# A long causal convolution with top-128 routing on one core: a wider unit memory, weighted sums in two accumulators, contiguous copies, and every transfer on one queue

## The chip, the core and the metric

The kernel runs on one core of a Trainium2 chip. The core has a matrix engine (PE, whose weight loads are listed apart as PEld), a vector engine (DVE), an activation engine (ACT), a general engine (POOL) and a sync engine (SP) that only issues transfers. Each engine works through its own instructions in order and waits at semaphores for the others. The metric is the device time of one execution in microseconds; less is better.

## The reference, cut to what matters

```python
batch, seq, d_model = (8, 6336, 128)          # x: 8 x 6336 x 128, h: 6336 x 128
def _attn_ref(x, h):                          # causal convolution along the sequence, per feature
    L = 2 * S
    Xf = np.fft.rfft(x, n=L, axis=1)
    Hf = np.fft.rfft(h, n=L, axis=0)
    return np.fft.irfft(Xf * Hf[None], n=L, axis=1)[:, :S, :]
def _moe_ref(x, w_gate, w1, w2, capacity):    # capacity 128, w1: 128 x 1024, w2: 1024 x 128
    scores = np.einsum('bsd,d->bs', x, w_gate)
    out = x.copy()
    for b in range(B):
        top_idx = np.argpartition(-scores[b], capacity)[:capacity]
        xe = x[b, top_idx]
        ye = np.maximum(xe @ w1, 0.0) @ w2
        g = 1.0 / (1.0 + np.exp(-scores[b, top_idx]))
        out[b, top_idx] = x[b, top_idx] + g[:, None] * ye
    return out
```

The convolution of eight sequences with one filter per feature comes first. Then, for each sequence, the 128 rows with the highest gate score go through a small two-layer network and are written back.

## The kernel before

The sequence length is 6336 = 99 * 64, and the transforms are done as matrix products with tables, in fp32, first over 99 points and then over 64. The work is cut into eight **units**: unit i holds two sequences (2 * (i // 2) and the next) and one half of the features (64 columns). All units go through the same four stages:

- **stage a** (`stage_a`, L121): a group of input columns, folded by POOL (`fold`, L108 and L109: two tensor operations per group), times the table `fa`; the result leaves PSUM by two ACT copies (L127) and two DVE copies (L129) into the unit's spectrum `ys`. Eight groups per unit. The PSUM tiles come from the pool `pb`, which has two buffers.
- **stage b** (`stage_b`, L153): for a chunk of eight of the 99 frequencies, `over_k` multiplies the spectrum by the table `wb` (64 PE instructions per full chunk, into a `pb` tile); then `times` multiplies by the filter's spectrum: four DVE products (L161) out of PSUM, and two POOL additions (L171), which write the result back into the same place of the spectrum. Thirteen chunks per unit, the last one of three frequencies.
- **stage c** (`stage_c`, L231): 64 columns of the spectrum times the table `wc` (16 PE instructions for every two of the 66 steps), and ACT copies (L236), four columns at a time, into `z`. In the same loop DVE adds up the **weighted sum** of all columns (`weigh`, L208 and L210), from which the gate scores come.
- **stage d** (`stage_d`, L264): 16 items of eight PE instructions with the table `at`, one ACT copy each (L269), and one store of the output.

Spectrum, z and the table chunks of stage b share one tile, `slots`, of two slots. Unit i uses slot i % 2: the spectrum lies in the last 12672 numbers of a lane's 16384, z overwrites it from the front while stage c consumes it, and the first 3072 numbers hold three chunks of `wb`:

```python
flat = cp.tile([128, 2 * ZS], F32, name="slots")
ys = [flat[:, (r + 1) * ZS - YS:(r + 1) * ZS].rearrange("p (j k t) -> p j k t", k=N1, t=2) for r in range(2)]
zs = [flat[0:N1, r * ZS:(r + 1) * ZS].rearrange("p (j m t) -> p j m t", m=128, t=2) for r in range(2)]
```

The order of the work is written out by hand, and a layer below it adds a semaphore wait wherever two instructions touch the same part of a tile. First come stage a of the filter and of unit 0, then stage b of both, chunk by chunk (`stage_b_first`, which also copies the filter's spectrum by ACT, L192, and stores it by ACT's queue, L198). From there on, unit i runs stages c and d while unit i + 1 runs stages a and b: the 33 **items** of unit i (17 of stage c with four steps each, 16 of stage d) are emitted one after the other, and ahead of items 1, 3, 5 and 7 stand two groups of stage a, ahead of items 10, 14, 18, 22 and 26 a **pair** of chunks of stage b, ahead of item 30 the last three. After every item one step of the **routing** is emitted (`routes`): scores (L288), a search for the threshold in 16 rounds of one small matmul (L345) and some DVE work (L333 to L350), the gather, and the network for the picked rows (L461, L469). A pair of sequences is complete after two units, so the search runs in stage d of units 1, 3, 5 and 7, and what is left of the routing in stage c of units 2, 4 and 6, and after the last unit.

Two details of the order matter below. `weigh` is emitted ahead of step s until `2 * s + 6` columns are weighed, so all 64 stand in the first half of stage c. And the transfers stand in two queues: SP issues all loads (`load_x` L101, `load_w` L139, `load_h` L145, `load_at` L247), and ACT, between its copies, the output stores (L274, one item late by way of `flush`) and the stores of L198. Each of eight semaphores for transfers is used in turn, so the ninth transfer waits for the first one's end.

## Time and profile before

| | |
|---|---|
| three runs | 1562.04, 1570.03 (median) and 1576.72 us |
| profiled execution | 1568.27 us, of which the span from the first to the last instruction is 1566.5 us |
| mean granted clock of PE | 0.79 of full speed |
| busy share of the span | PE 72%, PEld 62%, DVE 51%, POOL 29%, ACT 21% |
| moved by DMA | 170.81 MB, 109 GB/s over the span |

The span has these stretches: 0 to 51 us stage a of the filter and unit 0; 51 to 137 us the first stage b; then unit by unit stage c and stage d, beginning with unit 0 (137 to 231 and 231 to 308 us); the last unit has nothing to prepare (1434 to 1466 and 1466 to 1521 us), and the last routing ends at 1566.5 us. A share of busy time over the whole span says little here, since the stretches have different limits. What a stretch is worth is read from its own windows and waits.

### The profile page before, as it was taken

To read this page: it belongs to the slowest core of one execution; us is meant where nothing else is said; L and a number is where in the kernel's file an instruction comes from. 1 tells how busy PE (TensorE), PEld (TensorE's weight loads), DVE (VectorE), ACT (ScalarE), POOL (GpSimd) and SP (SyncE) were. 2 spreads that over 40 slices of the span, in tenths; PEclk is the share of its full clock that TensorE was granted. 3 is DMA by queue.
4 is the path that set the end of the run, shared out by engine and by line. 5 is a ranking of instruction groups with operands and counts; after the bars stand their busy time and mean duration, and the time that the engine had idled before them with its cause. 6 is when DMAs were issued, how large, how long until landed. Compare 5 with 4: busy or idle time off the path is not lost.

```text
span 1566.5 us, 39581 instructions
## 1 busy us (share of the span) xinstructions
PE 1122.1 (72%) x17336; PEld 967.9 (62%) x17336; DVE 797.1 (51%) x1927; ACT 329.6 (21%) x603; POOL 459.7 (29%) x371
## 2 busy tenths in 40 slices
PE   6766676767777677766776857767776776777984
PEld 5665575557556576556755757656755666666754
DVE  5436823483466822266274863238446584236552
ACT  3211221132111221123210222103311122113310
POOL 4334323342223233242223223333222223331001
PEclk8997798888775788988886678888888577888855
DMA  7574235432444223542352422434244401252120
GB/s 243 165 236 138 82 86 165 126 121 79 119 120 125 70 58 100 165 140 81 93 148 74 128 59 83 128 112 152 81 114 133 125 18 46 69 166 69 51 83 7
DMA packets 102344, 170.81 MB, mean 109 GB/s; under 512 B 10814, under 2 KB 80028, under 8 KB 102172
## 3 DMA queue, kind: packets, MB, share of 16 engines
q1 hardware_dynamic: 67324, 134.79, 29.0%
q10 hardware_dynamic: 33824, 32.45, 6.6%
q8 instruction: 136, 2.23, 0.6%
q0 software_dynamic: 1024, 1.05, 0.3%
q14 instruction: 36, 0.29, 0.1%
HBM read 135.29 MB, written 32.96 MB: 107 GB/s over the span
## 4 chain that ended last, share of the span: by engine, by line
PE 53%; DVE 26%; POOL 12%; issue 5%; DMA 2%; ACT 1%; POOLq 0%; SPq 0%; DVEq 0%; ACTq 0%
PE pb L153 17%; PE pa L264 17%; DVE acc L210 14%; PE pa L231 11%; POOL slots L171 10%; PE pb L121 4%; DVE slots L129 3%; DVE tx L161 3%; PE m L461 1%; PE m L469 1%; DVE cmp L333 1%; DMA at<-tab_at 1%; POOL xr L109 1%; DVE slots L161 1%; DVE num L337 1%
## 5 line engine op out<-in xcount | busy, mean ns | idle before, releaser
L153 PE MATMUL pb<-slots 128*64 128x64 f32 x6336 | 282.2, 262 | 242.4 <-POOL slots L171 242.3
L171 POOL TENSOR_TENSOR slots<-slots,tx 128x512 f32<-128x512 f32 (+1 forms) x208 | 265.4, 1297 | 629.9 <-DVE tx L161 620.9
L153 PEld LDWEIGHTS pb<-slots 128*64 128x64 f32 x6336 | 265.4, 176 | 260.8 <-POOL slots L171 251.0
L161 DVE TENSOR_TENSOR slots<-pb,ht 128x512 f32<-128x512 f32 (+1 forms) x182 | 120.2, 660 | 437.4 <-PE pb L153 437.2
L264 PE MATMUL pa<-slots,at 99*99 99x256 f32 (+1 forms) x1056 | 310.3, 456 | 8.8 <-ACT slots L236 4.9
L231 PE MATMUL pa<-wc,slots 64*99 64x128 f32 x4096 | 301.7, 304 | 2.3 <-POOL slots L171 1.8
L231 PEld LDWEIGHTS pa<-wc,slots 64*99 64x99 f32 x4096 | 282.3, 191 | 18.1 <-issue 9.0
L210 DVE SCALAR_TENSOR_TENSOR acc<-slots,wgl,acc 128x198 f32<-128x198 f32 x504 | 276.7, 550 | 19.6 <-POOL slots L171 3.4
L264 PEld LDWEIGHTS pa<-slots,at 99*99 99x99 f32 x1056 | 201.0, 203 | 88.4 <-DMA at<-tab_at 7.6
L121 PE MATMUL pb<-fa,xr 50*64 50x99 f32 x2304 | 159.0, 296 | 131.8 <-DVE slots L129 81.1
L236 ACT COPY slots<-pa 99x512 f32<-99x512 f32 x256 | 160.0, 629 | 408.7 <-PE pa L231 393.6
L121 PEld LDWEIGHTS pb<-fa,xr 50*64 50x64 f32 x2304 | 136.7, 167 | 148.3 <-issue 98.5
L269 ACT COPY yt<-pa 99x512 f32<-99x512 f32 x128 | 75.0, 586 | 589.3 <-PE pa L264 314.6
L121 PE MATMUL pb<-fa,xo 50*64 50x99 f32 x2304 | 157.8, 297 | 2.1 <-issue 2.1
L121 PEld LDWEIGHTS pb<-fa,xo 50*64 50x64 f32 x2304 | 133.7, 166 | 2.2 <-issue 2.2
L108 POOL TENSOR_TENSOR xo<-xr 128x512 f32<-128x512 f32 x55 | 71.2, 1294 | 200.4 <-PE pb L121 200.4
L161 DVE TENSOR_TENSOR tx<-pb,ht 128x512 f32<-128x512 f32 (+1 forms) x182 | 119.0, 654 | 0.0
L129 DVE COPY slots<-pb 128x396 f32<-128x396 f32 x144 | 74.9, 563 | 81.0 <-PE pb L121 81.0
L109 POOL TENSOR_TENSOR xr<-xr 128x512 f32<-128x512 f32 x72 | 91.6, 1273 | 33.1 <-DVE xo L108 27.4
L127 ACT COPY slots<-pb 128x396 f32<-128x396 f32 x144 | 66.9, 522 | 122.9 <-PE pb L121 122.9
L435 POOL DMA_INDIRECT xe<-out,iu x16 | 16.1, 1008 | 154.3 <-DVE col L424 151.9
L333 DVE SCALAR_TENSOR_TENSOR cmp<-r,q,quarters 99x192 bf16<-99x192 f32 x128 | 54.7, 469 | 0.3
(95 smaller groups left out, 448.4 us busy)
## 6 DMA issues: line engine op xcount, KB each, us to landing
slots<-tab_wb SPq DMA_DIRECT2D x96, 512.0 KB
xr<-in_x SPq DMA_DIRECT2D x64, 512.0 KB
out<-yt ACTq DMA_DIRECT2D x128, 198.0 KB
ht<-hd SPq DMA_DIRECT2D x84, 256.0 KB
at<-tab_at SPq DMA_DIRECT2D x128, 153.1 KB
hd<-slots ACTq DMA_DIRECT2D x24, 256.0 KB
xr<-in_h SPq DMA_DIRECT2D x8, 512.0 KB
slots<-tab_wb SPq DMA_DIRECT2D x8, 192.0 KB
```

The source lines that it names most:

```text
L108: eng.tensor_tensor(out=odd[g], in0=t[:, 1], in1=t[:, 0], op=ALU.subtract)
L109: pool.tensor_tensor(out=t[:, 0], in0=t[:, 0], in1=t[:, 1], op=ALU.add)
L121: pe.matmul(pt[c * 64:c * 64 + 64, b, d * N1:(d + 1) * N1], src, fa[rows, c], start=True, stop=True)
L129: v.tensor_copy(out=dst[:, b, j:j + 2], in_=src[:, b])
L153: pe.matmul(banks[c][g * 64:g * 64 + 64, j * 64:j * 64 + 64], wt[:, j, c * 64:c * 64 + 64], y[:, :, g, :, k0 + j], start=True, stop=True)
L161: v.tensor_tensor(out=dst, in0=banks[c][:, 0:kn * 64].rearrange("p (k b j t) -> p k b j t", k=kn, b=2, t=2), in1=ht[t].rearrange("p k (j t ...
L171: pool.tensor_tensor(out=d3, in0=d3, in1=tx.rearrange("p k (j t) -> p k j t", t=2), op=ALU.add if c else ALU.subtract)
L210: v.scalar_tensor_tensor(out=acc[:, b], in0=col, scalar=w, in1=acc[:, b], op0=ALU.mult, op1=ALU.add)
L231: pe.matmul(banks[g][0:N1, c % 4 * 128:c % 4 * 128 + 128], y[rows, c // 2, ri, :, c % 2], wc[rows, ri], start=(ri == 0), stop=(ri == 1))
L236: act.copy(out=z[:, c // 2 - 1:c // 2 + 1, g].rearrange("p j m t -> p j t m"), in_=banks[g][0:N1].rearrange("p (j t m) -> p j t m", j=2, t=2))
L264: pe.matmul(pt[0:N1, o:o + w * 128], ats[tau // 2][:, tau % 2, c], z[:, c, q:q + w], start=(c == 0), stop=(c == 1))
L269: act.copy(out=yt.rearrange("p b q d -> p q b d"), in_=pt[0:N1].rearrange("p (q b d) -> p q b d", q=4, b=2))
```

## The change

Six things change.

1. The tile `slots` gets 100 more numbers (400 bytes) in each lane. Nothing is stored in them.
2. `acc` is doubled: columns of even and odd number (t = 0 and 1) are added up in sums of their own, and the scores' first matmul (`scores`) adds the two, with 16 PE instructions in the place of eight.
3. `weigh` is emitted until `s + 5` columns are weighed, one per step, so the 64 are spread over 59 of the 66 steps.
4. z of four columns is one run of 512 numbers rather than two of 256, by another order of the features (`_features`, on the host's side of the layout); so g = 0 no longer holds back its last copy.
5. The products `tx` have three buffers rather than two.
6. The output stores and the stores of the filter's spectrum are issued by SP rather than ACT. They keep their places in the program's order.

```diff
-    flat = cp.tile([128, 2 * ZS], F32, name="slots")
+    flat = cp.tile([128, 2 * ZS + 100], F32, name="slots")
...
-    acc = cp.tile([128, 2, 2, N1], F32, name="acc")
+    acc = cp.tile([128, 2, 2, 2, N1], F32, name="acc")
...
-            tx = tp.tile([128, KC, 64], F32, tag="t", name="tx", bufs=2)[:, 0:kn]
+            tx = tp.tile([128, KC, 64], F32, tag="t", name="tx", bufs=3)[:, 0:kn]
...
-            act.dma_start(out=hd[u, :, :, k0:k0 + kn], in_=hs[:, :, u, 0:kn])
+            sp.dma_start(out=hd[u, :, :, k0:k0 + kn], in_=hs[:, :, u, 0:kn])
...
-        if u == 0 and d == 0:
-            v.tensor_scalar(out=acc[:, b], in0=col, scalar1=w, scalar2=None, op0=ALU.mult)
+        dst = acc[:, t, b]
+        if u == 0 and d < 2:
+            v.tensor_scalar(out=dst, in0=col, scalar1=w, scalar2=None, op0=ALU.mult)
         else:
-            v.scalar_tensor_tensor(out=acc[:, b], in0=col, scalar=w, in1=acc[:, b], op0=ALU.mult, op1=ALU.add)
+            v.scalar_tensor_tensor(out=dst, in0=col, scalar=w, in1=dst, op0=ALU.mult, op1=ALU.add)
...
-        z = zs[r].rearrange("p (j g) m t -> p j g m t", g=2)
+        z = zs[r].rearrange("p (n g j) m t -> p n g j m t", g=2, j=2)
...
-            while weighed < min(64, 2 * s + 6):
+            while weighed < min(64, s + 5):
...
-                c = cols[g] if s < 63 else 63 if s == 65 else -1
+                c = cols[g]
                 if 0 <= c < 64 and c % 4 == 3:
-                    act.copy(out=z[:, c // 2 - 1:c // 2 + 1, g].rearrange("p j m t -> p j t m"),
+                    act.copy(out=z[:, c // 4, g].rearrange("p j m t -> p j t m"),
...
-                act.dma_start(out=out[2 * p:2 * p + 2, u, :, 4 * n:4 * n + 4].rearrange("b a q d -> a b q d"), in_=yt)
+                sp.dma_start(out=out[2 * p:2 * p + 2, u, :, 4 * n:4 * n + 4].rearrange("b a q d -> a b q d"), in_=yt)
...
-                pe.matmul(pt[0:N1, b * 128:(b + 1) * 128], acc[:, b, ri], wc[:, ri], start=(ri == 0), stop=(ri == 1))
+                for t in range(2):
+                    pe.matmul(pt[0:N1, b * 128:(b + 1) * 128], acc[:, t, b, ri], wc[:, ri],
+                              start=(ri + t == 0), stop=(ri + t == 2))
```

What this does to the order shows at three places. The first is the pair of chunks of stage b ahead of item 10 of unit 0, on PE (`pb` is the PSUM tile of a chunk, the names in brackets are the semaphores waited for: DMAHW for a load, DVE and Pool for those engines). Before:

```order
L153 MATMUL pb<-slots 64x64 [waits DMAHW6_49,DVE_49]
L153 MATMUL pb<-slots 64x64 [waits DVE_49]
L153 MATMUL pb<-slots 64x64 x30
L153 MATMUL pb<-slots 64x64 [waits DMAHW7_49,Pool_49]
L153 MATMUL pb<-slots 64x64 x31
```

Now:

```order
L153 MATMUL pb<-slots 64x64 [waits DMAHW6_49]
L153 MATMUL pb<-slots 64x64 [waits DVE_49]
L153 MATMUL pb<-slots 64x64 x30
L153 MATMUL pb<-slots 64x64 [waits DMAHW7_49]
L153 MATMUL pb<-slots 64x64 x31
```

The second chunk waited for POOL, which writes the first chunk's result into other frequencies of the same spectrum; it now waits for its load alone. The same wait is gone from every chunk of the kernel; where a `pb` tile is still in use, the wait is for DVE's products of the chunk before the last.

The second place is DVE's queue in the front of stage c of unit 0: the weighings (L210 before, L211 now) around the copies of the last two stage a groups (ahead of item 7), up to the first product of stage b (ahead of item 10). Before:

```order
L210 SCALAR_TENSOR_TENSOR acc<-slots,wgl,acc 128x198 [waits DVE_49] x16
L129 COPY slots<-pb 128x2x2x99 [waits PE_49]
L129 COPY slots<-pb 128x2x2x99
L129 COPY slots<-pb 128x2x2x99 [waits PE_49]
L129 COPY slots<-pb 128x2x2x99
L210 SCALAR_TENSOR_TENSOR acc<-slots,wgl,acc 128x198 [waits DVE_49] x4
L161 TENSOR_TENSOR slots<-pb,ht 128x8x32x2 [waits DMAHW1_49,PE_49,Activation_49]
L161 TENSOR_TENSOR tx<-pb,ht 128x512
```

Now (L209 begins a new sum):

```order
L211 SCALAR_TENSOR_TENSOR acc<-slots,wgl,acc 128x198 [waits DVE_49] x8
L129 COPY slots<-pb 128x2x2x99 [waits PE_49]
L129 COPY slots<-pb 128x2x2x99
L129 COPY slots<-pb 128x2x2x99 [waits PE_49]
L129 COPY slots<-pb 128x2x2x99
L209 TENSOR_SCALAR acc<-slots,wgl 128x198 x2
L211 SCALAR_TENSOR_TENSOR acc<-slots,wgl,acc 128x198 [waits DVE_49] x10
L161 TENSOR_TENSOR slots<-pb,ht 128x8x32x2 [waits DMAHW7_49,PE_49,Activation_49]
```

Ahead of these copies stand eight weighings where 16 stood. Before, all 64 were done ahead of the first product of stage b; now 44 are, 16 more stand between the first pair of chunks and the second, and the last four behind that.

The third place is SP's queue in stage d of unit 0, from a pair of chunks on. Before:

```order
L139 DMA slots<-tab_wb 128x1024 [waits DMAHW6_49,PE_49]
L145 DMA ht<-hd 128x2x256 [waits DMAHW7_49,DMAHW0_49,DVE_49]
L139 DMA slots<-tab_wb 128x1024 [waits DMAHW0_49,PE_49]
L145 DMA ht<-hd 128x2x256 [waits DMAHW3_49,DMAHW2_49,DVE_49]
L247 DMA at<-tab_at 99x396 [waits DMAHW3_49,PE_49]
L247 DMA at<-tab_at 99x396 [waits DMAHW5_49,DMAHW1_49,PE_49]
```

Now:

```order
L139 DMA slots<-tab_wb 128x1024 [waits DMAHW6_49,PE_49]
L145 DMA ht<-hd 128x2x256 [waits DMAHW7_49,DVE_49]
L139 DMA slots<-tab_wb 128x1024 [waits DMAHW0_49,PE_49]
L145 DMA ht<-hd 128x2x256 [waits DMAHW1_49,DVE_49]
L248 DMA at<-tab_at 99x396 [waits DMAHW2_49,PE_49]
L275 DMA out<-yt 99x2x256 [waits DMAHW3_49,Activation_49]
L248 DMA at<-tab_at 99x396 [waits DMAHW4_49,PE_49]
L275 DMA out<-yt 99x2x256 [waits DMAHW5_49,Activation_49]
```

A store that waits for an ACT copy now stands between every two loads of `at`.

4 lines of the change are left out of this document (2 added, 2 removed).

## The prediction

> **What bounds the kernel now.** I read the chain of work that ended last first (section 4 of the page), then a table of windows by stage, then the waits, then timelines of PE and DVE in the stages that the chain names. The chain's shares by engine and line:
>
> ```profile
> PE 53%; DVE 26%; POOL 12%; issue 5%; DMA 2%; ACT 1%; POOLq 0%; SPq 0%; DVEq 0%; ACTq 0%
> PE pb L153 17%; PE pa L264 17%; DVE acc L210 14%; PE pa L231 11%; POOL slots L171 10%; PE pb L121 4%; DVE slots L129 3%; DVE tx L161 3%; PE m L461 1%; PE m L469 1%; DVE cmp L333 1%; DMA at<-tab_at 1%; POOL xr L109 1%; DVE slots L161 1%; DVE num L337 1%
> ```
>
> PE does not lead alone: POOL's additions of stage b (L171) and DVE's weighings (L210) stand on the path with 24% between them. The windows by stage show how long each stretch is (length, then busy time of PE, PEld, DVE, ACT, POOL, then the granted clock and the DMA share):
>
> ```profile
> 51.00:137.00 86.00, 54.44 (x1596) 52.45 (x1587) 32.47 (x57) 13.96 (x28) 32.47 (x26) 0.92 0.58 188
> 231.00:308.00 77.00, 54.27 (x669) 43.59 (x669) 25.48 (x43) 9.28 (x16) 24.94 (x20) 0.84 0.45 131
> 308.00:395.00 87.00, 62.09 (x1280) 58.01 (x1280) 51.31 (x90) 27.75 (x49) 28.53 (x22) 0.84 0.38 114
> 395.00:492.00 97.00, 69.88 (x692) 55.03 (x693) 53.66 (x178) 9.10 (x16) 25.01 (x20) 0.72 0.37 106
> 492.00:604.00 112.00, 80.20 (x1352) 72.82 (x1351) 65.14 (x161) 30.32 (x59) 34.63 (x28) 0.76 0.31 89
> 1434.00:1466.00 32.00, 31.09 (x515) 29.67 (x513) 23.32 (x56) 20.56 (x33) 0.00 (x0) 1.00 0.11 32
> ```
>
> These are the first stage b, stage d of unit 0, stages c and d of unit 1 (d with the search), stage c of unit 2 (with the rest of the routing), and stage c of unit 7, which has neither stage a nor b beside it and no POOL work. There the 512 instructions of stage c take 32 us at full clock; beside stages a and b the same work takes 87 to 112 us, with PE busy 62 to 80. In every stretch before the last unit some 20 us or more of PE are idle. The waits say where:
>
> ```profile
> PE pb L153 <- POOL slots L171: 242.3, 61, 5.9
> PE pb L121 <- DVE slots L129: 81.1, 20, 5.4
> ```
>
> **The wait for POOL.** A pair of chunks in stage c of unit 1, and one in stage d of unit 0, on PE (start, length, count, and in brackets the idle time ahead with its releaser):
>
> ```profile
> 362.65 2.10 PE L153 MATMUL pb<-slots 128*64 128x64 f32 x64
> 369.02 3.53 PE L153 MATMUL pb<-slots 128*64 128x64 f32 x64 [4.27 <-POOL slots L171]
> 372.49 7.58 PE L231 MATMUL pa<-wc,slots 64*99 64x128 f32 x128
> 379.99 2.10 PE L153 MATMUL pb<-slots 128*64 128x64 f32 x64
> ...
> 257.92 3.68 PE L153 MATMUL pb<-slots 128*64 128x64 f32 x64 [4.18 <-POOL slots L171]
> 261.53 7.96 PE L264 MATMUL pa<-slots,at 99*99 99x256 f32 x32
> 269.42 2.10 PE L153 MATMUL pb<-slots 128*64 128x64 f32 x64
> ```
>
> The second chunk waits some 4.2 us for products and additions of the first, and then runs 3.53 to 3.68 us where the first ran 2.10: the pause has halved the clock. So a removed wait is worth 4.2 us plus about 1.4 of slow clock, 5.6 us. The order shows that the change removes it everywhere (the 61 waits are 12 in the first stage b and seven in each of units 0 to 6). What comes next is the second chunk's load, issued two chunks earlier, and the `pb` tile, free since the chunk before the last.
>
> In the first stage b the wait is shorter, once per chunk:
>
> ```profile
> 59.38 2.10 PE L153 MATMUL pb<-slots 128*64 128x64 f32 x64 [2.37 <-POOL slots L171]
> 61.32 2.04 PE L153 MATMUL pa<-slots 128*64 128x64 f32 x64
> ```
>
> Twelve of 2.37 us are 28 us. DMA moves there at a share of 0.58 of 86 us, 50 us of work, which the shorter stretch must still hold with the spectrum's stores now in one queue with the loads. I take **22 us** (ends: 0 if the transfers bind at today's pace, 36 if PE's 50 us alone do).
>
> In stage d the three pairs and the last three chunks of a unit lose 3 x 5.6 + 2 x 4.2 + 1.4 = 26.6 us; seven units, **186 us**. DVE (four products a chunk) and POOL hide under the items of stage d that follow.
>
> **The front of stage c.** DVE leads there. One cycle of two items in unit 1 and, by its copies alone, in unit 2:
>
> ```profile
> 329.08 10.20 DVE L210 SCALAR_TENSOR_TENSOR acc<-slots,wgl,acc 128x198 f32<-128x198 f32 x16
> 339.20 1.04 DVE L129 COPY slots<-pb 128x396 f32<-128x396 f32 x2
> 342.07 1.05 DVE L129 COPY slots<-pb 128x396 f32<-128x396 f32 x2 [1.83 <-PE pb L121]
> 343.03 10.11 DVE L210 SCALAR_TENSOR_TENSOR acc<-slots,wgl,acc 128x198 f32<-128x198 f32 x16
> ...
> 516.61 1.04 DVE L129 COPY slots<-pb 128x396 f32<-128x396 f32 x2
> 532.83 1.04 DVE L129 COPY slots<-pb 128x396 f32<-128x396 f32 x2
> ```
>
> Weighings alone in unit 7, and the line's shortest, median and longest (ns):
>
> ```profile
> 1435.91 23.32 DVE L210 SCALAR_TENSOR_TENSOR acc<-slots,wgl,acc 128x198 f32<-128x198 f32 x51
> ```
> ```profile
> L210 DVE SCALAR_TENSOR_TENSOR acc<-slots,wgl,acc x504: 406/425/1541, 139.4 to 1458.8; 128x198 f32<-128x198 f32 x168
> ```
>
> The cycle is 343.03 - 329.08 = 13.95 us, 16.2 with routing. A weighing costs 0.457 us with POOL idle (23.32 / 51), of which a part is the wait for the one before it, since all add to one sum; the 16 of a cycle take 10.20 us, not 7.3, because POOL's four folds run meanwhile: single weighings then last up to 1541 ns. The copies, which PE waits for, stand behind them. Two sums take some of the dependence away; no row shows weighings without it. I bound the new step by the shortest one, 0.406, and today's 0.457, and take 0.42. Eight fewer weighings are 3.7 us and the shorter step 0.3: 4.0 us a cycle in the four units without routing, where the folds still block the eight that stay. With routing DVE spends more of the cycle on other work, so I let half of the blocking (1.45 of 2.9 us) go as well: 5.5 us. Four cycles each: 4 x 4 x 4.0 + 3 x 4 x 5.5 = **130 us** (ends: 0 if DVE's other work fills the room; 190 if no fold blocks any more, when copies of 2.1, PE's 1.8 and eight weighings of 0.406 make a cycle of 7.2 us, 6.8 less, in 28 cycles).
>
> **The back of stage c.** From pair to pair is 379.99 - 362.65 = 17.34 us today. Without the wait PE needs 2 x 2.1 + 7.58 = 11.8. But DVE now has 16 weighings between the pairs, and POOL's additions meet them:
>
> ```profile
> L161 DVE TENSOR_TENSOR slots<-pb,ht 128x512 f32<-128x512 f32 (+1 forms) x182 | 120.2, 660 | 437.4 <-PE pb L153 437.2
> L171 POOL TENSOR_TENSOR slots<-slots,tx 128x512 f32<-128x512 f32 (+1 forms) x208 | 265.4, 1297 | 629.9 <-DVE tx L161 620.9
> ```
>
> Eight products of 0.66, 16 x 0.42, and one POOL addition of 1.3 that is still running when the weighings begin: 13.3 us. The z copies wait for weighings, so PE follows: 17.3 - 13.3 = 4.0 us a pair, 14 pairs, **56 us** (ends: 0, and 5.6 x 14 = 78). Here a rule speaks against the change. The Trainium skill (SBUF — State Buffer, section Who interferes with whom) says that a DVE instruction with two SBUF inputs contends with a POOL instruction that reads SBUF, and that the later one waits until the earlier is done. The maximum of L210 agrees with it: 1541 ns is 1135 over the minimum, less than one POOL operation of 1297. If all eight additions of the two pairs blocked by that rule rather than two, the sum would be 7 x 6 x 1.3 = 55 us longer.
>
> **The search in stage d.** Units 1, 3 and 5, on PE:
>
> ```profile
> 452.98 1.96 PE L264 MATMUL pa<-slots,at 99*99 99x256 f32 x8
> 457.53 0.24 PE L345 MATMUL m<-num,ones 99*99 99x6 bf16 x1 [2.60 <-DVE num L337]
> 457.63 3.71 PE L264 MATMUL pa<-slots,at 99*99 99x256 f32 x8
> ```
>
> Unit 7's search, as a window:
>
> ```profile
> 1480.00:1500.00 20.00, 20.00 (x52) 13.10 (x52) 9.62 (x48) 2.93 (x5) 0.00 (x0) 0.50 0.35 99
> ```
>
> A pause of 2.6 us doubles an item from 1.96 to 3.71 us, and in unit 7 the clock stays at 0.50. Some nine of 16 items run so today; two chunks of stage b in one run of PE should keep more of them fast. I take six items of 1.65 us in three units, **30 us** (ends 0 and 45). Against it, the search's DVE work queues behind eight products (5.3 us) while PE needs 4.2 + 2 for the pair and an item: 1.5 us at four places in three units, **18 us** lost.
>
> **Transfers and the rest.** SP now issues a store between any two loads. A store waits for a copy that is one item old, so it should hold nobody; what it costs ACT today is 0.3 us each, in idle time:
>
> ```profile
> L274 ACTq DMA_DIRECT2D out<-yt x128: 302/303/617, 245.1 to 1522.1; - x128
> ```
> ```profile
> 246.27 4.28 DMA at<-tab_at
> ```
>
> The second row, from the chain, shows that a late load of `at` can cost 4.3 us. Stage d of unit 0 has DMA at 0.45 of 77 us, 35 us, to fit into some 50. I take 3 us a unit, **21 us** lost (ends 0, and 4.3 at each of four places of seven units, 120).
>
> ```profile
> L288 PE MATMUL m<-wc,acc 128*99 128x128 f32 x32 | 4.1, 272 | 0.0
> L236 ACT COPY slots<-pa 99x512 f32<-99x512 f32 x256 | 160.0, 629 | 408.7 <-PE pa L231 393.6
> ```
>
> The scores' matmuls double, **4 us** lost. The contiguous z copies move as many numbers as before, and ACT stands idle 408.7 us ahead of them: 0, or a tenth of 160 us either way if that cover goes. The third `tx` buffer is wanted only where chunks follow closely; DVE paces POOL there (2.6 us a chunk each): 0.
>
> The sum: 22 + 186 + 130 + 56 + 30 - 18 - 21 - 4 = 381 us. The profiled execution took 1568.3 us (span 1566.5), 1.8 below the median of 1570.0; I stay with it: **1187 us**.
>
> **The rivals.** (1) DVE and POOL take POOL's place: all weighings still go past all of POOL's work, the back of stage c gains nothing (56) and the front half (65): 1308 us. For it speaks that DVE is busy 51 of 87 us in c, against it that PE is busy 62. The skill's rule above gives 1242 on this path. (2) The clock stays low: every second chunk still runs slow (1.4 us at two places in c and four in d, seven units, 59) and the 30 of the search fail: 1276. (3) The clock recovers by itself. The Trainium skill (TensorE: Matmul & The Clock Gate, Part 1) says that some 3.4 us of sustained work lift the clock; the row at 1480 us, busy 20 of 20 at 0.50, disagrees. As a mechanism here, the last unit's 16 items would run at 1.96 rather than 3.71: 28 us less, 1159. (4) DVE and DMA hide better than costed: without the 18, the 21 and with the back at 78: 1126. (5) The waits vanish but the time is bound by what they hid, so that only the front's 130 us come: 1438. The 20 us and more of PE idle in every stretch speak against it. (6) Slower: SP's single queue. Each store held until its copy is done holds the next load; if each of 128 items then waits 4.28 us as at 246 us, that is 548 us, 1735. It decides from 381 / 128 = 3.0 us a store. Today SP is ahead by four `at` tiles, so this is unlikely.
>
> **How the numbers follow.** My forecast has 0.62, the rivals 0.13, 0.08, 0.04, 0.07, 0.03 and 0.03 in their order. The forecast alone I hold good to 1120 to 1260. The range from 1110 to 1300 takes in (2), (3), (4), the skill's price and most of (1), and leaves out the upper part of (1), (5) and (6). About 1% is what a measurement tells from no change here. Faster by over 1%: all but (6) and some tail of (5), 0.95; within 1%: that tail, 0.02; slower: (6), 0.03.
>
> **What would show it.** Right: no wait of L153 for L171; L153 mostly at 2.1 us per 64; stage d of unit 0 at 50 to 58 us, of unit 1 at 60 to 72; stage c of unit 1 at 58 to 68 and of unit 2 at 78 to 90; a mean clock near 0.9. Wrong: L121 or L231 waiting for DVE as long as now; weighings with a mean above 0.55 us; PE waiting for `at` or for `wb`; stage d with the search still at a clock near 0.7.

## The result and the profile after

The changed kernel takes 1175.9 us (median of 1164.96 to 1196.97, four runs), the one before 1567.9 on the same occasion (1562.04 to 1576.72). The ratio is 0.747, with a 95% interval of 0.739 to 0.755. This ratio and those below leave out runs that lie more than 1.5% above the fastest of the same kernel, here the one of 1196.97 us. The profiled execution of the changed kernel took 1170.5 us, with a span of 1168.7 us and a mean granted clock of 0.89. Below, stages are timed from their first to their last PE instruction.

The chain that ended last, by engine and by line:

```profile
PE 51%; DVE 33%; issue 7%; DMA 4%; POOL 3%; ACT 2%; SPq 0%; POOLq 0%; ACTq 0%; DVEq 0%
PE pa L232 13%; PE pa L265 12%; PE pb L153 10%; PE pb L121 9%; DVE acc L211 7%; DVE tx L161 7%; DVE slots L161 5%; DMA at<-tab_at 3%; DVE cmp L336 3%; PE pa L153 2%; DVE num L340 2%; PE m L472 2%; DVE slots L129 2%; PE m L464 2%; POOL xr L109 1%
```

POOL's additions (L171), 10% of the chain before, no longer stand in this list, and the weighings fell from 14% to 7%. The products of stage b (L161) grew from 4% to 12% in their two forms, and the search's compare (L336) from 1% to 3%: DVE is now waited for in stage d. The same stretches as before, as windows (length; busy PE, PEld, DVE, ACT, POOL; clock; DMA share; GB/s):

```profile
51.00:112.70 61.70, 50.15 (x1610) 48.72 (x1604) 33.19 (x57) 14.11 (x28) 32.81 (x25) 0.97 0.76 244
171.00:226.60 55.60, 48.92 (x668) 39.19 (x668) 22.19 (x40) 10.02 (x17) 23.09 (x20) 0.94 0.55 168
226.60:284.50 57.90, 53.06 (x1282) 48.97 (x1280) 47.64 (x94) 27.23 (x47) 30.46 (x24) 1.00 0.58 185
284.50:361.50 77.00, 64.29 (x701) 50.29 (x701) 55.60 (x177) 10.32 (x18) 25.16 (x20) 0.78 0.41 124
361.50:453.00 91.50, 70.97 (x1350) 64.98 (x1351) 64.12 (x166) 29.70 (x59) 35.43 (x29) 0.85 0.38 119
1057.00:1088.30 31.30, 31.17 (x515) 29.70 (x513) 21.16 (x64) 20.29 (x33) 0.00 (x0) 1.00 0.11 35
1088.30:1123.60 35.30, 31.78 (x165) 22.80 (x165) 29.26 (x141) 9.31 (x16) 0.00 (x0) 1.00 0.48 138
```

These are the first stage b, stage d of unit 0, c and d of unit 1, c of unit 2 up to its stage d, and c and d of unit 7. Stage c of unit 1 went from 87 us with a clock of 0.84 to 58 at full clock: its idle PE fell from 25 us to 5. Stage d of unit 1, with the search, still has 13 us of idle PE and a clock of 0.78. What PE still waits for (total, times, longest):

```profile
PE m L348 <- DVE num L340: 41.2, 19, 3.6
...
PE pb L121 <- DVE slots L129: 14.9, 6, 3.5
...
PE pa L265 <- DMA at<-tab_at: 12.3, 12, 2.5
...
DVE acc L211 <- POOL slots L171: 7.9, 4, 2.0
```

The wait of L153 for L171 (242 us before) does not occur any more; the wait for the stage a copies fell from 81 to 15 us. The group of stage b's matmuls shows the clock that came back with it, 210 us for the same 6336 instructions, which took 282; first before, then now:

```profile
L153 PE MATMUL pb<-slots 128*64 128x64 f32 x6336 | 282.2, 262 | 242.4 <-POOL slots L171 242.3
L153 PE MATMUL pb<-slots 128*64 128x64 f32 x6336 | 210.1, 226 | 13.1 <-issue 7.9 <-PE pb L153 5.2
```

Where the time went, in us, by stages of both traces (PE's first to last instruction; the first row ends where stage c of unit 0 begins):

| | before | after | difference |
|---|---|---|---|
| up to the first stage c | 137.0 | 112.9 | -24.1 |
| stage c of units 0, 1, 3, 5 (no routing) | 353.3 | 226.0 | -127.3 |
| stage c of units 2, 4, 6 (routing) | 331.6 | 253.3 | -78.3 |
| stage d of units 0, 2, 4, 6 | 317.2 | 215.7 | -101.5 |
| stage d of units 1, 3, 5 (search) | 288.9 | 219.8 | -69.1 |
| stage c and d of unit 7 | 86.1 | 65.6 | -20.5 |
| between stages, and the end | 52.4 | 75.4 | +23.0 |

Together -397.8 us, the difference of the two spans (1566.5 and 1168.7).

### The profile page after: what moved, and what is told of

Same layout as the page of the kernel before. It is cut to its first block, busy times and chain, and to the rows that moved or that the text cites. A ratio compares the mean times of both kernels' runs of the same rounds, so it can differ in the third digit from the quotient of the medians.

```text
span 1168.7 us, 39686 instructions
## 1 busy us (share of the span) xinstructions
PE 983.2 (84%) x17368; PEld 851.8 (73%) x17368; DVE 761.9 (65%) x1927; ACT 330.0 (28%) x603; POOL 462.7 (40%) x371
## 4 chain that ended last, share of the span: by engine, by line
PE 51%; DVE 33%; issue 7%; DMA 4%; POOL 3%; ACT 2%; SPq 0%; POOLq 0%; ACTq 0%; DVEq 0%
PE pa L232 13%; PE pa L265 12%; PE pb L153 10%; PE pb L121 9%; DVE acc L211 7%; DVE tx L161 7%; DVE slots L161 5%; DMA at<-tab_at 3%; DVE cmp L336 3%; PE pa L153 2%; DVE num L340 2%; PE m L472 2%; DVE slots L129 2%; PE m L464 2%; POOL xr L109 1%
## 5 line engine op out<-in xcount | busy, mean ns | idle before, releaser
L171 POOL TENSOR_TENSOR slots<-slots,tx 128x512 f32<-128x512 f32 (+1 forms) x208 | 266.0, 1312 | 370.6 <-DVE tx L161 367.8
L265 PE MATMUL pa<-slots,at 99*99 99x256 f32 (+1 forms) x1056 | 278.1, 420 | 22.0 <-DMA at<-tab_at 12.3
L232 PE MATMUL pa<-wc,slots 64*99 64x128 f32 x4096 | 273.3, 286 | 12.5 <-ACT slots L237 6.2
L232 PEld LDWEIGHTS pa<-wc,slots 64*99 64x99 f32 x4096 | 253.0, 175 | 26.4 <-ACT slots L237 6.8
L265 PEld LDWEIGHTS pa<-slots,at 99*99 99x99 f32 x1056 | 183.5, 186 | 84.8 <-DMA at<-tab_at 17.4
L211 DVE SCALAR_TENSOR_TENSOR acc<-slots,wgl,acc 128x198 f32<-128x198 f32 x496 | 229.6, 532 | 7.9 <-POOL slots L171 7.9
L153 PE MATMUL pb<-slots 128*64 128x64 f32 x6336 | 210.1, 226 | 13.1 <-issue 7.9
L153 PEld LDWEIGHTS pb<-slots 128*64 128x64 f32 x6336 | 201.3, 141 | 25.7 <-issue 17.2
L161 DVE TENSOR_TENSOR slots<-pb,ht 128x512 f32<-128x512 f32 (+1 forms) x182 | 119.5, 656 | 141.7 <-PE pb L153 117.4
L121 PE MATMUL pb<-fa,xr 50*64 50x99 f32 x2304 | 142.9, 276 | 59.2 <-POOL xr L109 32.4
L270 ACT COPY yt<-pa 99x512 f32<-99x512 f32 x128 | 75.1, 587 | 398.1 <-PE pa L265 181.3
L121 PEld LDWEIGHTS pb<-fa,xr 50*64 50x64 f32 x2304 | 123.7, 153 | 73.5 <-POOL xr L109 35.8
L121 PE MATMUL pb<-fa,xo 50*64 50x99 f32 x2304 | 142.0, 276 | 1.8 <-issue 1.8
L161 DVE TENSOR_TENSOR tx<-pb,ht 128x512 f32<-128x512 f32 (+1 forms) x182 | 118.8, 653 | 1.2 <-POOL slots L171 1.2
L336 DVE SCALAR_TENSOR_TENSOR cmp<-r,q,quarters 99x192 bf16<-99x192 f32 x128 | 56.8, 485 | 0.3
```

The lines of the kernel that those rows point to most:

```text
L121: pe.matmul(pt[c * 64:c * 64 + 64, b, d * N1:(d + 1) * N1], src, fa[rows, c], start=True, stop=True)
L153: pe.matmul(banks[c][g * 64:g * 64 + 64, j * 64:j * 64 + 64], wt[:, j, c * 64:c * 64 + 64], y[:, :, g, :, k0 + j], start=True, stop=True)
L161: v.tensor_tensor(out=dst, in0=banks[c][:, 0:kn * 64].rearrange("p (k b j t) -> p k b j t", k=kn, b=2, t=2), in1=ht[t].rearrange("p k (j t ...
L171: pool.tensor_tensor(out=d3, in0=d3, in1=tx.rearrange("p k (j t) -> p k j t", t=2), op=ALU.add if c else ALU.subtract)
L211: v.scalar_tensor_tensor(out=dst, in0=col, scalar=w, in1=dst, op0=ALU.mult, op1=ALU.add)
L232: pe.matmul(banks[g][0:N1, c % 4 * 128:c % 4 * 128 + 128], y[rows, c // 2, ri, :, c % 2], wc[rows, ri], start=(ri == 0), stop=(ri == 1))
```

## The experiments

Twelve kernels ran, each against the kernel before on the same chip. They ask three things: what each part is worth, what the last unit's clock has to do with it, and what is left in stage d.

### The 100 numbers alone

The kernel before, with one edit:

```diff
-    flat = cp.tile([128, 2 * ZS], F32, name="slots")
+    flat = cp.tile([128, 2 * ZS + 100], F32, name="slots")
```

> The kernel before with the tile slots 400 bytes a lane wider, and nothing else. Theory: the width alone frees the chunks of stage b from the wait for POOL. Then the first stage b ends near 113 us, stage d of unit 0 takes about 54 us, a pair of chunks in stage c some 11.8 us to the next pair (no weighings stand there), while the front of stage c keeps its cycle of 14 us, because its weighings are where they were: 1568 less 24, 186, 78 and 12 is about 1268 us (1240 to 1300). Rival: the order of DVE's work is what counts, and without the later weighings little comes of it: over 1400 us.

Measured: 1317.9 us (1309.96 to 1336.53), ratio 0.838 (0.828 to 0.849). The windows of stage c and d of unit 1, and then two of its waits:

```profile
250.10:331.00 80.90, 61.96 (x1282) 57.84 (x1280) 56.13 (x96) 27.70 (x49) 30.32 (x24) 0.83 0.42 130
331.00:405.20 74.20, 61.18 (x693) 47.66 (x694) 55.63 (x178) 9.16 (x16) 25.04 (x20) 0.81 0.47 139
```
```profile
PE pb L121 <- DVE slots L129: 86.6, 22, 5.4
...
PE pa L264 <- DMA at<-tab_at: 29.7, 12, 3.0
```

The wait of L153 for POOL is gone here too, and with it 256 us, the larger part of the change. (Some 20 us of these are stage d of unit 7, 35.7 us here and 55.4 before, which has no stage b beside it; it is taken up below.) The time is some 50 us above the expected one and above its range. The waits did go, but stage d of units 0 to 6 gained 147 us in the place of 186: the table is late there (29.7 us; 3.9 before), and the search runs at a clock of 0.81. The stage a copies still stand behind the weighings (86.6 us), as expected. The runs show that the width does it. Why the layer that adds the waits takes two chunks for the same part of the tile at the one width and not at the other, no run shows; no third width was tried.

### Everything but the 100 numbers

```diff
-    flat = cp.tile([128, 2 * ZS + 100], F32, name="slots")
+    flat = cp.tile([128, 2 * ZS], F32, name="slots")
```

> The changed kernel with the tile slots as narrow as before. Theory: L153 waits some 240 us for L171 again, and only the front of stage c gains: its cycle falls from 14 to 7.5 us in the four units without routing and by some 5 us in the others, 28 cycles, 160 to 180 us: 1390 to 1410 us. Rival: if the other five edits carry the gain, it stays under 1300 us; if they are worth nothing without the width, it is 1540 us or more.

Measured: 1425.2 us (1420.51 to 1428.81), ratio 0.906 (0.899 to 0.914). The wait is back, and stage d of the even units takes 76 to 80 us (76 to 82 before); stage c takes 68 to 70 without routing. The time is 15 us above the expected range:

```profile
L153 PE MATMUL pb<-slots 128*64 128x64 f32 x6336 | 280.2, 261 | 240.9 <-POOL slots L171 240.9
```

The 100 numbers are worth 249 us on top of the rest (1425.2 - 1175.9) and 256 alone (1574.3, the median of the kernel before on that chip, - 1317.9), so the parts hardly overlap.

### One sum

The changed kernel with all weighings in one sum:

```diff
-    acc = cp.tile([128, 2, 2, 2, N1], F32, name="acc")
+    acc = cp.tile([128, 2, 2, N1], F32, name="acc")
...
-        dst = acc[:, t, b]
-        if u == 0 and d < 2:
+        dst = acc[:, b]
+        if u == 0 and d == 0:
```

> The changed kernel with one sum in the place of two (the scores with eight matmuls again). Theory: a weighing starts every 0.335 us with two sums and every 0.46 us with one, and DVE sets the front's cycle (weighings 4.3, copies 2.1, a wait of 1.1 us in 7.5 us): 8 x 0.12 is 1 us a cycle in 28 cycles, and up to 2 us at each of 14 places in the back: 1200 to 1225 us. Rival: PE's own 7 us set the cycle and the longer weighings are hidden: within 10 us of 1176.

Measured: 1212.5 us (1209.19 to 1228.64), ratio 0.770 (0.763 to 0.778): 37 us more, in the expected range. The weighings of unit 7, which has no POOL work, first with two sums (the changed kernel), then with one (timeline of DVE: start, length, count):

```profile
1056.59 21.57 DVE L211 SCALAR_TENSOR_TENSOR acc<-slots,wgl,acc 128x198 f32<-128x198 f32 x64 [1.98 <-POOL slots L171]
```
```profile
1099.20 29.34 DVE L211 SCALAR_TENSOR_TENSOR acc<-slots,wgl,acc 128x198 f32<-128x198 f32 x64 [1.99 <-POOL slots L171]
```

A weighing costs 21.57 / 64 = 0.337 us where the sum was last written two weighings earlier, and 29.34 / 64 = 0.458 where it was written by the one just before.

### The weighings early

The changed kernel, two sums kept, with the old place of the weighings:

```diff
-            while weighed < min(64, s + 5):
+            while weighed < min(64, 2 * s + 6):
```

> The changed kernel with weighings emitted as early as before (2 s + 6), in two sums. Theory: the front's cycle is DVE's: 16 weighings (5.4 us and 3 us behind folds), copies and their wait, 11.7 us where it is 7.5, 28 cycles, 118 us; the back keeps its 11.4 us, which is PE's own work: 1270 to 1300 us. Rival: two sums already make DVE fast enough, and where the weighings stand matters little: under 1210 us.

Measured: 1209.3 us (1205.0 to 1229.93), ratio 0.768 (0.760 to 0.775). The theory fell and the rival, that two sums suffice for DVE to keep up, held. DVE in the front of stage c of unit 1:

```profile
242.91 1.04 DVE L129 COPY slots<-pb 128x396 f32<-128x396 f32 x2
245.78 1.05 DVE L129 COPY slots<-pb 128x396 f32<-128x396 f32 x2 [1.83 <-PE pb L121]
246.74 6.58 DVE L211 SCALAR_TENSOR_TENSOR acc<-slots,wgl,acc 128x198 f32<-128x198 f32 x16
253.25 1.03 DVE L129 COPY slots<-pb 128x396 f32<-128x396 f32 x2
```

Sixteen weighings take 6.58 us here and took 10.11 in one sum; the cycle is 253.25 - 242.91 = 10.3 us. Of the 33 us over the changed kernel some 20 are the last unit's stage d (55.0 us against 34.9), which has no part in this edit and is taken up below. So either of the two edits alone gets most of what both get: the run with the 100 numbers alone, which has neither, took 1317.9 us.

### The stores back on ACT

```diff
-            sp.dma_start(out=hd[u, :, :, k0:k0 + kn], in_=hs[:, :, u, 0:kn])
+            act.dma_start(out=hd[u, :, :, k0:k0 + kn], in_=hs[:, :, u, 0:kn])
...
-                sp.dma_start(out=out[2 * p:2 * p + 2, u, :, 4 * n:4 * n + 4].rearrange("b a q d -> a b q d"), in_=yt)
+                act.dma_start(out=out[2 * p:2 * p + 2, u, :, 4 * n:4 * n + 4].rearrange("b a q d -> a b q d"), in_=yt)
```

> The changed kernel with both kinds of stores back on ACT's queue; everything else stays. The changed kernel is at 1175.9 us. Theory: which queue issues the stores changes nothing, since a store costs its engine 0.3 us (128 x 0.3 = 38 us on ACT, which is idle more than two thirds of the time) and SP runs ahead of its loads by four tiles of the table: 1166 to 1186 us. Rival 1: the stores on SP hold the loads behind them (PE waits for the table of stage d in 12 places, 12.3 us in all, three times what it was before), so that moving them back gains 10 to 20 us: 1156 to 1166. Rival 2: ACT is wanted for z and the output copies now that the rest is faster, so that moving them back costs: over 1186 us.

Measured: 1197.4 us (1190.89 to 1209.31), ratio 0.763 (0.757 to 0.770), some 21 us more. The theory, that the queue does not matter, fell. The time is that of rival 2, but not for its reason. Stage c, where ACT copies z, takes 55 to 59 us without routing (55 to 58 with the stores on SP); the first stage c begins at 114.1 us (112.9), so that the stores of the first stage b matter little. It is stage d of units 0, 2, 4 and 6 that takes 58 to 64 us rather than 52 to 55 in the traced execution, the longest of the four (1209.3 us), and there the table is late:

```profile
PE pa L265 <- DMA at<-tab_at: 30.8, 12, 3.4
```

The same wait is 12.3 us with the stores on SP, and 11.3 to 16.8 in the six other runs here that have them there with the 100 numbers and with pairs. The kernel before with the 100 numbers, whose stores are ACT's too, has 29.7. A reading of the queues, not tried by itself: with stores between its loads SP is held back by them; without them its loads of stage b run further ahead, and the table's loads land later.

### z strided, and two tx buffers

The changed kernel with the older z (and order of the features), and with two tx buffers:

```diff
-        z = zs[r].rearrange("p (n g j) m t -> p n g j m t", g=2, j=2)
+        z = zs[r].rearrange("p (j g) m t -> p j g m t", g=2)
...
-            tx = tp.tile([128, KC, 64], F32, tag="t", name="tx", bufs=3)[:, 0:kn]
+            tx = tp.tile([128, KC, 64], F32, tag="t", name="tx", bufs=2)[:, 0:kn]
```

> The changed kernel with z laid out as before (two runs of 256 numbers, the older order of the features, the last copy of one half held back to the end of stage c) and with two tx buffers. Theory: neither part does anything, since the z copy lasts 633 ns in the changed kernel and 627 in the one before, and ACT is idle ahead of it: 1168 to 1184 us. Rival: the copy that is held back delays the first item of stage d by some 2 us in each of eight units, or POOL's additions wait for a free tx: 1185 to 1200 us.

Measured: 1195.5 us (1187.66 to 1201.52), ratio 0.763 (0.756 to 0.769), which is the rival's number. So tx was tried alone, with only its line of the diff above:

> The changed kernel with two tx buffers rather than three, all else as changed, to tell which part of the strided-z run's 20 us is z and which is tx. Theory: the third tx buffer does nothing, since PE waits for a pb tile and not for tx, and the 20 us were mostly the last unit's stage d at a low clock (50 us rather than 35): 1166 to 1186 us. Rival: with two, DVE's products wait for POOL's additions of a pair, which hold back the search or the weighings behind them: 1186 to 1200 us.

Measured: 1176.6 us (1172.98 to 1179.58), ratio 0.752 (0.744 to 0.760): the third buffer does nothing, as expected. That left 19 us for z, or for the last unit. Stage d of unit 7 with the strided z, in three windows around PE's wait, and the same stage in the changed kernel:

```profile
1106.00:1110.00 4.00, 3.02 (x16) 2.05 (x14) 3.04 (x14) 1.17 (x2) 0.00 (x0) 1.00 0.45 110
1110.00:1120.00 10.00, 9.12 (x26) 6.16 (x27) 6.58 (x31) 1.17 (x2) 0.00 (x0) 0.59 0.34 100
1120.00:1130.00 10.00, 10.00 (x27) 6.62 (x26) 5.44 (x27) 1.76 (x3) 0.00 (x0) 0.50 0.38 108
```
```profile
1096.00:1100.00 4.00, 2.13 (x11) 1.36 (x10) 3.83 (x17) 0.59 (x1) 0.00 (x0) 1.00 0.38 109
1100.00:1110.00 10.00, 10.00 (x50) 6.83 (x49) 9.83 (x53) 3.23 (x6) 0.00 (x0) 1.00 0.61 171
```

In both, PE waits 1.9 us for the first step of the search. With the strided z the clock then falls to 0.50 and an item takes 3.7 us; in the changed kernel it stays at 1.00 and an item takes 2.0. To tell this from z, the strided-z kernel got seven matmuls whose results nobody reads, ahead of the first step of each of unit 7's two searches:

```diff
                 pt = psm()
+                if phase[0] == 7 and it == 0:
+                    for _ in range(7):
+                        pe.matmul(pt[0:N1, 256:512], acc[:, 0, 0, 0], wc.rearrange("p c n -> p (c n)"),
+                                  start=True, stop=True)
```

> The strided-z run's kernel (1195.5 us) with seven matmuls of 256 columns, whose results nobody reads, on PE ahead of the first step of each of the two searches in stage d of unit 7, so that PE's wait for DVE there (1.9 us) is filled with work. In the strided-z run the clock falls to 0.50 at that wait and stays there for 35 us, so that unit 7's stage d takes 50 us; with three tx buffers and contiguous z, or with two tx buffers and contiguous z, the same wait of 1.9 us is followed by a clock of 1.00 and 35 us. Theory: it is this wait, after which the clock falls in some programs and not in others, and not z that makes most of the strided-z run's 19 us over the run with two tx buffers: without the wait, unit 7's stage d takes 34 to 37 us at a clock of 1.00, and the kernel 1176 to 1184 us. Rival 1: the clock falls there without the wait as well, for some other reason: 50 us and 1192 to 1200. Rival 2: the wait goes and z's own cost is spread over the other units: stage d of unit 7 at 35 us, but the whole at 1188 or more.

Measured: 1174.4 us (1172.6 to 1180.81), ratio 0.750 (0.746 to 0.755), 21 us less than without the idle work. Stage d of unit 7:

```profile
1091.00:1128.30 37.30, 37.30 (x193) 27.47 (x193) 29.26 (x141) 8.80 (x15) 0.00 (x0) 1.00 0.46 130
```

PE is busy in all 37.3 us, at full clock. The time even ends a little below the theory's 1176. So z's layout does nothing measurable; the wait of 1.9 us and the clock behind it made the strided-z run's 19 us.

### Single chunks

The changed kernel with the chunks of stage b spread out, none added or taken away:

```diff
-                for n in range(6):
-                    plan.setdefault(10 + 4 * n, []).append(("b", 2 * n))
+                for n, at in enumerate((8, 10, 12, 14, 16, 18, 20, 22, 24, 26, 28, 29, 30)):
+                    plan.setdefault(at, []).append(("b", n))
...
-                        for ci in (n, n + 1) if n < 10 else (10, 11, 12):
-                            stage_b(i + 1, ci)
+                        stage_b(i + 1, n)
```

> The changed kernel with the chunks of stage b emitted one by one, at items 8, 10, 12 and so on to 30, rather than in pairs ahead of every fourth item. No work is added or taken away. Theory: in stage d of units 1, 3 and 5 the matrix engine waits 2.1 to 3.6 us at the places after a pair, because a step of the search stands on DVE behind eight products (4.9 us), and the clock then drops; four products take 2.5 us, about as long as PE's chunk and item, so these waits go and with them the slow clock: stage d with the search at 58 to 62 us rather than 72 to 75, 3 x 13 = 39 us less, about 1135 us (1120 to 1150). Rival 1: the search is bound by its own chain, so that stage d stays at 70 us or more: 1165 to 1180. Rival 2: single chunks meet the weighings in more places, and the back of stage c gets slower by a POOL addition (1.3 us) at each of seven units' chunks: over 1180 us.

Measured: 1111.4 us (1105.98 to 1118.5), ratio 0.711 (0.706 to 0.717), better than both kernels and than expected. Stages d of unit 0 and unit 1 as windows, and the search's wait:

```profile
172.50:217.00 44.50, 44.28 (x604) 34.94 (x604) 22.96 (x38) 8.96 (x16) 24.94 (x20) 1.00 0.66 204
...
278.50:343.50 65.00, 53.32 (x638) 41.95 (x638) 58.21 (x178) 9.00 (x16) 26.04 (x20) 0.92 0.47 143
```
```profile
PE m L348 <- DVE num L340: 44.9, 26, 2.9
```

The theory was right about the place and wrong about the mechanism. The search's waits did not go: they are 44.9 us in 26 pieces, where they were 41.2 in 19. Many are shorter, though, 1.3 to 1.4 us, and the clock holds at 0.92 where it was 0.78 (1.00 and 0.97 in units 3 and 5, where it was 0.81); that is 31 us in the three units with the search, some 6 of them for one chunk a unit (2.1 us) that has moved to stage c. Short waits alone do not explain it: in unit 3 the clock stays at 1.00 behind waits of 2.9 and 2.6 us as well. Another 33 us was in neither expectation: stage d of units 0, 2, 4 and 6 takes 44 to 46 us rather than 52 to 55, PE busy all along at full clock, some 8 us for the chunk that has moved, the rest with a table that is never late, now that the loads of stage b come one by one; and the pauses between stages shrink by 20 us. Stage c takes 14 us longer in all, with five chunks in it rather than four, and stage d of unit 7 takes 8 us longer.

### The step first

The changed kernel, pairs kept, with a routing step of stage d emitted ahead of the chunks and the item:

```diff
+                if item == 17:
+                    phase[1] = True
+                if phase[1]:
+                    next(routes, None)
...
-                if item == 17:
-                    phase[1] = True
                 next(strand, None)
-                next(routes, None)
+                if not phase[1]:
+                    next(routes, None)
```

> The changed kernel with the routing's step emitted ahead of the chunks and of the item of stage d, rather than after them; the pairs stay pairs and stage c is as it was. Theory, as for the single chunks: what makes PE wait in the search is that the step which follows a pair stands on DVE behind the pair's eight products. Ahead of them it is done by the time PE asks for it, and the step behind the pair has two items of time: the waits of 2.1 to 3.6 us go, stage d of units 1, 3 and 5 at 58 to 64 us, 1130 to 1145 us in all. Rival: a step takes DVE some 2 us after its matmul whatever stands ahead, about as long as an item, so that PE waits at every item instead: stage d stays at 70 us or more, 1165 us or more.

Measured: 1146.8 us (1141.79 to 1186.52), ratio 0.732 (0.726 to 0.739). Stage d of units 1, 3 and 5 takes 63 to 66 us, close to the theory, but not in its way. The waits did not go: in unit 1 they are 3.8, 2.1 and 3.1 us, where they were 3.6, 2.1 and 3.3, because the step emitted after the pair and one item still stands on DVE behind the pair's eight products. What fell is the time that PE takes for the same items. Those of unit 1, in the changed kernel and then in this run (busy us, mean ns, idle time ahead of them):

```profile
L265 PE MATMUL pa<-slots,at 99*99 99x256 f32 (+1 forms) x132 | 42.0, 481 | 2.3 <-ACT slots L237 2.3
L265 PE MATMUL pa<-slots,at 99*99 99x256 f32 (+1 forms) x132 | 34.9, 418 | 0.0
```

In the three units that is 121.9 and 107.4 us, at a clock of 0.78, 0.81 and 0.81 and then of 0.92, 0.87 and 0.87. Another 9 us are the scores' matmuls (L290): they are emitted earlier here and run in the pause ahead of the stage, where PE waited 2.3 us for the last copy of z. In the changed kernel the clock is 0.50 for 6.8 us at that wait; here it stays at 1.00. In the search it is 0.50 for a shorter time behind the same waits, and why the run does not show. The pause ahead of stage d of units 2, 4 and 6, whose routing steps moved too, grew from 5 to 6 us to 9 to 10.

Both edits together, the step first only in the units with the search:

> Single chunks as in the run with single chunks (1111.4 us), and the search's step ahead of the chunk and of the item in stage d of units 1, 3, 5 and 7. Theory: what is left of PE's waits in the search with single chunks, 1.3 to 1.4 us after each chunk, is the step behind four products; ahead of them it has two items of time. Five waits of 1.4 us in three units are 21 us, so stage d with the search goes from 61 to 65 us to 55 to 58, and the time to 1085 to 1100 us. Rival: the step's own chain (matmul to DVE's compare to the next matmul) is longer than an item of 2.0 us, so that the waits move to the items without a chunk: 1105 to 1118 us.

Measured: 1108.1 us (1098.6 to 1122.14), ratio 0.711 (0.701 to 0.720), no different from single chunks alone. The theory fell; the time is the rival's. Its timeline in stage d of unit 1 suggests why. One step's compares in the item before a chunk's additions, then a step beside them:

```profile
302.54 0.75 DVE L336 SCALAR_TENSOR_TENSOR cmp<-r,q,quarters 99x192 bf16<-99x192 f32 x2
...
305.82 2.79 POOL L171 TENSOR_TENSOR slots<-slots,tx 128x512 f32<-128x512 f32 x2 [4.92 <-DVE tx L161]
...
306.98 1.84 DVE L336 SCALAR_TENSOR_TENSOR cmp<-r,q,quarters 99x192 bf16<-99x192 f32 x2
```

The compares take 0.75 us alone and 1.84 beside POOL, 1.1 us more, somewhat less than one of POOL's additions (two in 2.79 us); with that a step is longer than an item of 1.95 us, and without it shorter. The next experiment asked whether that is for their two inputs from SBUF:

```diff
-                    v.scalar_tensor_tensor(
-                        out=cmp[:, j], in0=r[:, j].unsqueeze(1).broadcast_to([N1, 3, N2]), scalar=q[:, j:j + 1],
-                        in1=quarters[0:N1], op0=ALU.subtract, op1=ALU.is_ge)
+                    for k in range(3):
+                        v.tensor_scalar(out=cmp[:, j, k], in0=r[:, j], scalar1=q[:, j:j + 1], scalar2=0.25 * (k + 1),
+                                        op0=ALU.subtract, op1=ALU.is_ge)
```

> As the last run of single chunks with the step first (1108.1 us), with the search's compare split: rather than one DVE operation with two inputs from SBUF for a sequence (the remainders, and a table of quarters), three with one input and the quarter as a constant. In that last run two compares take 0.75 us with POOL idle and 1.84 us beside POOL's additions, and PE then waits 1.4 us. Theory: an operation with two SBUF inputs is held until POOL's operation is done, one with a single input is not; so the six compares take the same time, some 1.0 to 1.3 us, with POOL as without it, the waits after a chunk shrink to some 0.8 us, and stage d with the search goes from 63 to about 60 us: 1090 to 1105 us. Rival 1: POOL slows every DVE operation, so that the six also stretch, by the length of an addition or more: 1108 to 1125 us. Rival 2: the compares were not what PE waits for, and four more instructions a step cost 0.5 us in 64 steps: 1110 to 1140 us.

Measured: 1123.5 us (1121.63 to 1132.69), ratio 0.720 (0.714 to 0.727). The same places in its timeline:

```profile
302.21 1.07 DVE L337 TENSOR_SCALAR cmp<-r,q 99x64 bf16<-99x64 f32 x6
...
306.69 2.19 DVE L337 TENSOR_SCALAR cmp<-r,q 99x64 bf16<-99x64 f32 x6
```

The six stretch by 1.1 us, as the two did: rival 1's time, and half of its reason. Taking the second input away is therefore not enough. Yet not every DVE operation is slowed. The reduction (L340), with one input from SBUF as well, runs after POOL's additions in the timelines above, but six of the changed kernel's 64 run beside one, and all 64 take the same time (shortest, median and longest in ns):

```profile
L340 DVE TENSOR_REDUCE num<-cmp x64: 552/553/554, 303.8 to 1126.7; 99x6 bf16<-99x384 bf16 x64
```

The Trainium skill (SBUF — State Buffer, section Who interferes with whom) says that copies and tensor_scalar operations can also take the port pair that DVE shares with POOL, if their operands meet certain conditions, while a tensor_reduce on this chip never does. The six compares, 1.07 us alone and 2.19 beside POOL, and the reductions agree with it.

## Why the prediction was right, and where it was not

The time of 1175.9 us lies 11 us under the forecast of 1187, well inside the range; the forecast's own case came. That the sum came out so close is in part luck, as the last rows show. Step by step, against the profiled executions:

| step | predicted | measured |
|---|---|---|
| first stage b | -22 | -24 |
| stage c, front and back | -130 - 56 = -186 | -127.3 - 78.3 = -206 |
| stage d, units 0, 2, 4, 6: waits, less transfers | -4 x 23.6 = -94 | -101 |
| stage d, units 1, 3, 5: waits, search, transfers, scores | 3 x (-26.6 - 10 + 6 + 3 + 1) = -80 | -69 |
| stage d of unit 7 | 0 | -20 |
| between stages and the end | 0 | +23 |

**The waits of stage b for POOL** were the core, and they held. All 61 are gone, the second chunk of a pair runs at full clock, and the 100 numbers alone give 256 us. Of the bounds that the prediction named, those of stage d of unit 0 and stage c of unit 2 were met (54.2 us of 50 to 58, 84.4 of 78 to 90); stage c of unit 1 ended just under its own, 56.9 us against 58 to 68, and stage d of unit 1 above, 75.1 us against 60 to 72.

**The front of stage c** was mis-sized in two terms. The step of a weighing, taken as 0.42 us between 0.406 and 0.457, is 0.337. The lower bound was not one: the shortest row, 406 ns, is the length of one instruction, and since 64 weighings in two sums take 21.57 us, successive ones overlap. And the folds stretch the weighings by half of what had been kept for it. DVE in the front of stage c of unit 1 of the changed kernel:

```profile
230.60 1.04 DVE L129 COPY slots<-pb 128x396 f32<-128x396 f32 x2
232.79 1.05 DVE L129 COPY slots<-pb 128x396 f32<-128x396 f32 x2 [1.15 <-PE pb L121]
233.75 4.25 DVE L211 SCALAR_TENSOR_TENSOR acc<-slots,wgl,acc 128x198 f32<-128x198 f32 x8
238.97 1.05 DVE L129 COPY slots<-pb 128x396 f32<-128x396 f32 x2 [0.96 <-PE pb L121]
...
255.97 1.05 DVE L129 COPY slots<-pb 128x396 f32<-128x396 f32 x2
```

Three cycles take 255.97 - 230.60 = 25.4 us, 8.5 each, where 9.95 was predicted (13.95 - 4.0), and DVE now waits for PE ahead of most of its copies. The folds still stretch the eight weighings, 4.25 us rather than 8 x 0.337 = 2.7, but by 1.5 us, where the prediction kept 2.9. With routing the stage gained 78 us, 12 less than the 90 predicted; that DVE's other work filled part of the room there is likely, but not shown.

**The back of stage c** gained more than the 4.0 us a pair. Two pairs in unit 1 on PE, and between them the weighings on DVE:

```profile
263.64 3.98 PE L153 MATMUL pb<-slots 128*64 128x64 f32 x128
270.64 6.99 DVE L211 SCALAR_TENSOR_TENSOR acc<-slots,wgl,acc 128x198 f32<-128x198 f32 x16
275.09 3.98 PE L153 MATMUL pb<-slots 128*64 128x64 f32 x128
```

The pairs start 11.5 us apart, as PE alone needs (11.8 had been reckoned); 13.3 had been forecast. DVE takes 4.9 us for the eight products and 7.0 for the 16 weighings behind them, and its products follow 11.7 us apart, so it keeps pace with PE. Sixteen undisturbed weighings would take 5.4 us; POOL's additions beside them cost 1.6 us a pair, in DVE's time and hardly on the path. That they cost something agrees with the rule of the Trainium skill (SBUF — State Buffer, section Who interferes with whom) that spoke against the change, by which a DVE instruction with two SBUF inputs contends with a POOL instruction that reads SBUF. The 55 us that the prediction reckoned by it did not come, and rival 1 fell too.

**The search in stage d** is the step that failed, and in it the clock. The prediction let two chunks in one run of PE keep the clock up, and took 30 us off the items of stage d in units 1, 3 and 5 for it. They lost 6: they took 127.5 us before and take 121.9 now. Those of unit 1 before (42.0 now, as shown at the step first):

```profile
L264 PE MATMUL pa<-slots,at 99*99 99x256 f32 (+1 forms) x132 | 43.1, 491 | 1.0 <-ACT slots L236 1.0
```

The second chunks did better, L153 lost 23 us where 3 x (3 x 1.4 + 1.4) = 17 had been reckoned; the scores cost 7 us more rather than 3, in part since they run at the low clock behind the pause ahead of the stage (3.2 to 3.6 us a unit; 1.9 with single chunks). PE's idle time fell by 48 us, where 3 x 21 - 18 - 9 = 36 had been added up. The charge for the search behind eight products was about right: its waits (L345 before, L348 now) grew from 22.4 to 41.2 us in the whole kernel, 18.8 more, and 18 had been charged. PE in stage d of unit 1:

```profile
332.96 1.98 PE L265 MATMUL pa<-slots,at 99*99 99x256 f32 x8
...
334.81 1.96 PE L265 MATMUL pa<-slots,at 99*99 99x256 f32 x8
340.06 0.25 PE L348 MATMUL m<-num,ones 99*99 99x6 bf16 x1 [3.29 <-DVE num L340]
340.16 3.71 PE L265 MATMUL pa<-slots,at 99*99 99x256 f32 x8
```

The wait is 3.3 us (3.6 and 2.1 at the stage's two earlier ones), and the clock drops behind it as before, so that an item takes 3.71 us: the 30 us of search at a warm clock came only in part. Behind the eight products, DVE also changes here from the first search to the second, which is part of the 3.3 us. The step-first run shows that the items can lose another 14 us by the clock with the waits as they are; the timelines of the compare runs show that POOL's additions lengthen a step. Why the clock drops behind one wait and for how long stays open.

**Transfers and the queue.** 21 us were charged for crowding, and rival 6 held the single queue to be a danger. The crowding is there (PE waits 12.3 us for the table, 3.9 before), but the queue has the opposite sign: the stores on SP gain some 21 us against ACT, as the run with the stores back on ACT shows. The third tx buffer and the z copies cost and gain nothing, as costed.

**Two errors that cancelled.** Unit 7's stage d fell by 20 us, which the prediction gave no term but rival 3 a price of 28. No edit aims at it: both traces have the same wait of 1.9 us there, and the clock fell behind it in one and not in the other; for the forecast that is luck. Against it, the pauses between stages grew by 23 us in all; the prediction has no term for them. The pauses ahead of stage d of units 2, 4 and 6 are 13 us of this. In units 2, 4 and 6 a routing step stands behind weighings that POOL's additions hold. DVE and POOL before stage d of unit 2 of the changed kernel:

```profile
442.56 5.26 POOL L171 TENSOR_TENSOR slots<-slots,tx 128x512 f32<-128x512 f32 x4
...
444.57 4.49 DVE L211 SCALAR_TENSOR_TENSOR acc<-slots,wgl,acc 128x198 f32<-128x198 f32 x4
```

Four weighings take 4.49 us there and 1.35 elsewhere (4 x 0.337), and PE waits 4.2 us for the routing behind them.

## What to carry to other kernels

Look for waits that the data does not ask for: a dependence on another part of a shared tile cost this kernel about a sixth of its time, and a few unused bytes removed it. Once such a wait is gone, try the released work in small pieces rather than in runs of two or three: it gained another 64 us here, largely in stage d, where the table was no longer late and the clock in the search was higher. Price a wait on PE with the clock behind it, as a range and not as a number: in the changed kernel's search the clock was 0.50 behind every wait of 3.3 us and more, with single chunks it stayed at 1.00 behind one of 2.9. A stage's time that hangs on the clock behind one wait is no measure of an edit: fill the wait or compare the stages, as the strided z shows.
